# A Fourier layer with two feed-forward layers: the set-up ahead of the main loop written in another order, with four of its parts done in another way

## The chip, the cores and the metric

One NeuronCore of a Trainium2 chip. The metric is the time of one execution on the device, in microseconds (us), as the median over runs. The engines are called PE (TensorE), DVE (VectorE), ACT (ScalarE), POOL (GpSimd) and SP (SyncE, which only issues transfers here).

## The reference

```python
X = np.fft.fft(x, axis=1)          # x: (2, 3008, 256)
X = np.fft.fft(X, axis=2)
x = X.real.astype(np.float32).reshape(6016, 256)
h = x @ w_in                       # (256, 2048)
g = np.where(h >= 1, h, np.where(h <= -1, 0.0, (h + 1) ** 2 / 4))
x = (g @ w_out).astype(np.float32)
h = x @ w2_in
g = np.maximum(0.01 * h, h)
return (g @ w2_out).astype(np.float32)
```

The four weights arrive as float64 and are brought to float32 on the device, from their two 32-bit words. Every product with a main weight is made from a high and a low part of both factors (three products in place of one).

## The kernel before

**The set-up** (up to the first `step`) makes three things. (1) The first layer's weights w1 in 8 blocks: a load (`load_w1`, 512 KB), the conversion to float32 (`ToF32`: `begin` is two ACT passes, `exponent` one DVE pass L216, `join` two, `sign` L220 and `rest` L225), a product with the Fourier matrix of the 256 columns (`g_product`, PE), and the split of the result into high (`g_high`, ACT) and low (`g_low`, DVE) parts, `wa0` to `wa7`. (2) x, as 2 batches of 3 blocks: `load_x` brings one half of 512 KB by SP's queue, `add_x` adds the other half onto it by an accumulating transfer that POOL issues, `fold_x` (ten DVE passes and two or three on one column, L411 to L436) forms sums and differences. (3) The Fourier products over the 3008 positions: `even_product` (matrices `me0` to `me3`) and `odd_product` (matrices `mo0`, `mo1`), each in fp32 over the three blocks of a batch, into PSUM tiles `dc`/`ds` and `do`; then `odd_copy` and `odd_sum` join the odd halves, and `even_high`/`even_low`, `odd_high`/`odd_low` split all results into `bt0` to `bt7` (batch 0 has 0 to 3). The 129th frequency column goes other ways: `col_copy`, `col_even`, `col_even_out` (`ct` tiles by ACT), `col_row` (two row transfers out to DRAM and back spread over 128 partitions, issued by POOL), and for the weights `g_col` (many 2-column products) with `g_col_copy` into `g128`. `col_sign` flips signs in four `ct` tiles during later steps. `fill` and, in steps 1 to 3, the products into `full` serve no result.

**The main loop** has 128 steps of layer 1 and 128 of layer 2. Step n of layer 1 computes `p` (6 products), on DVE `aa`, two halves of `h` and a maximum `r`, on ACT three passes, then a high part `gh` (ACT) and a low part `gl` (POOL, L609); `second` of step n-4 (12 products into `acc`) follows `p` of step n on PE. The second weights w2 are converted too: blocks 0 to 3 in the set-up, 4 to 7 by a table of due steps (`plan_at`), with the low parts of 4 to 7 on POOL.

**The order** of the set-up is the list `ORDER`, written by hand: each item issues its instructions on its engines in turn, and every engine runs its own in that order. The tile pools add waits: a load into a reused buffer waits for the buffer's last reader. SP's loads are also numbered over eight completion counters, so that the ninth waits for the first to land, and so on; one waiting load holds back all behind it in SP's queue.

```python
def add_x(b, c):
    G.dma_start(out=xr[b, c], in_=xpq[b, c, 1], accum_op=ALU.add)
...
def sign(self):
    V.scalar_tensor_tensor(out=self.tmp, in0=self.high, scalar=-0x80000000, in1=self.tmp,
                           op0=ALU.bitwise_and, op1=ALU.bitwise_or)
```

Of the kernel before, what the change touches and what calls it, by code (L numbers as in the profile page):

```python
# [117 lines left out]
def _token_rows():  # L118

    i = np.arange(H4)  # L120
    rows = []
    for b in range(B):
        for k, neg in ((4 * i, 4 * (i + 1)), (4 * i + 2, 4 * i + 2),
                       (2 * i + 1, 2 * i + 1), (1503 - 2 * i, 1503 - 2 * i)):
            rows += [b * S + k, b * S + (S - neg) % S]
    return np.concatenate(rows)
# [4 lines left out]
load_w1 1, load_w1 4, load_x 0 0, load_cd, load_x 0 1, load_w1 2, load_x 0 2, w1_begin 1, load_w1 3,  # L131
w1_exponent 1, w1_begin 4, w1_join 1, w1_exponent 4, add_x 0 0, load_w1 0, g_product 1, fill 3, load_me 2,
w1_join 4, add_x 0 1, load_w1 6, g_product 4, fill 3, g_high 1, last_copy, load_me 3, load_mo 0, w1_begin 2,
g_low 1, load_mo 1, w1_exponent 2, g_high 4, add_x 0 2, w1_join 2, w1_begin 3, g_low 4, load_w1 7, g_product
2, fill 3, w1_exponent 3, w1_begin 0, w1_join 3, g_high 2, w1_exponent 0, load_w1 5, g_product 3, load_me 1,
g_low 2, w1_join 0, g_high 3, fold_x 0 0, g_product 0, w1_begin 6, g_high 0, g_low 0, load_x 1 0, col_copy 0
0, load_me 0, fold_x 0 1, even_product 0 1 0, g_col 1, load_w2 0, odd_product 0 0 0, g_col 4, w1_exponent 6,
even_product 0 1 1, g_col 2, col_copy 0 1, g_low 3, odd_product 0 0 1, w1_join 6, odd_product 0 1 0, g_col 0,
load_w2 1, fold_x 0 2, g_product 6, w1_begin 7, odd_product 0 1 1, g_high 6, w1_begin 5, w1_exponent 7,
odd_product 0 0 2, g_col 3, col_copy 0 2, g_low 6, w1_exponent 5, w1_join 7, add_x 1 0, odd_product 0 1 2,  # L140
g_col 6, odd_copy 0 0, w1_join 5, load_w2 2, load_x 1 1, odd_sum 0 0, load_w2 3, even_product 0 1 2, load_x 1
2, odd_high 0 0, odd_copy 0 1, g_product 5, odd_low 0 0, even_high 0 1, even_low 0 1, odd_sum 0 1,
even_product 0 0 0, g_high 5, fold_x 1 0, odd_high 0 1, even_product 0 0 1, add_x 1 1, even_product 0 0 2,
even_high 0 0, odd_low 0 1, odd_product 1 1 0, col_copy 1 0, even_low 0 0, add_x 1 2, col_row 0, odd_product 1 0 0, g_low
5, fold_x 1 1, even_product 1 0 0, g_col 5, g_product 7, fold_x 1 2, g_high 7, even_product 1 0 1, col_copy 1
1, odd_product 1 1 1, odd_product 1 0 1, g_low 7, w2_begin 0, even_product 1 0 2, g_col 7, w2_begin 1,
w2_exponent 0, col_copy 1 2, w2_exponent 1, col_even 0, even_high 1 0, w2_join 0, odd_product 1 0 2, even_low
1 0, col_even_out 0, w2_join 1, w2_begin 3, w2_exponent 3, w2_begin 2, even_product 1 1 0, odd_copy 1 0,
w2_exponent 2, odd_product 1 1 2, odd_sum 1 0, odd_high 1 0, odd_low 1 0, even_product 1 1 1, g_col_copy,
odd_copy 1 1, odd_sum 1 1, col_even 1, odd_high 1 1, odd_low 1 1, col_row 1, even_product 1 1 2, even_high 1 1, even_low  # L150
1 1, col_even_out 1, w2_high 0, step 0, w2_low 0, w2_high 1, w2_join 3, w2_low 1, w2_high 3, step 1,
w2_join 2, w2_low 3, w2_high 2, w2_low 2
# [5 lines left out]
def fnet_moe_kernel(ctx: ExitStack, tc: tile.TileContext, xpq, dft_e, dft_o, dft_d, pick,  # L158
# [39 lines left out]
    class ToF32:  # L198
# [4 lines left out]

        def load(self, w, j):
            self.raw = load_w(w, j)

        def begin(self):
# [15 lines left out]
        def rest(self):  # L223
            c = cv.tile([P, 512], I32, tag="cw", name="cw")
# [11 lines left out]
    def first_weights(j):  # L236
# [8 lines left out]
        def spill():  # L245
            c.rest()
# [45 lines left out]
        return ([("S", lambda: c.load(w3, j)), ("A", c.begin), ("V", c.exponent), ("V", c.sign), ("V", spill)],  # L292
# [3 lines left out]
    def second_weights(w, j, nm, engine, c):  # L296
# [6 lines left out]
        def low():  # L303
# [6 lines left out]

    with tc.manual_schedule():
# [5 lines left out]
        ev = pool("ev", 2, late, "right")  # L317
# [85 lines left out]
        def fold_x(b, c):  # L403
# [26 lines left out]
            x0, x1 = tc_[:, 2, P:P + 1], tc_[:, 3, P:P + 1]  # L430
            V.tensor_copy(tw_[:, 2, P - 1:P], x1)
            if c < 2:
                V.tensor_copy(tw_[:, 3, P - 1:P], x0)
            else:
                tt(tw_[:, 3, P - 1:P], x1, x0, ALU.subtract)
                V.scalar_tensor_tensor(out=tw_[:, 3, P - 1:P], in0=tw_[:, 3, P - 1:P], scalar=pk[:CH, 2:3],  # L436
                                       in1=x0, op0=ALU.mult, op1=ALU.add)
# [503 lines left out]
```

## Time and profile before

| | |
|---|---|
| median of 3 runs | 997.51 us (997.32 to 997.54) |
| the profiled execution: its time / its span | 996.57 us / 994.6 us |
| PE busy | 970.8 us (98%) |
| DVE / ACT / POOL busy | 63% / 71% / 50% |
| chain that ended last | PE 88%, DVE 6%, ACT 3%, DMA 2% |
| granted PE clock over the span | 0.995 |

The shares are means over a set-up of some 75 us and two long loops. The page's 40 slices show PE at 9 tenths in nearly all slices after the fifth; the first four hold the set-up, with DMA at 9, 9, 4, 2 tenths and DVE at 5 to 9. Times in the rows below are from the start of the span; a row of a timeline gives start, length, engine, line, operation, tiles and count, and in brackets the idle time before it and what ended it. A matmul of fp32 counts as two instructions in the trace.

### The profile page before, as it was taken

Reading aid. Unit: us, or ns where it says so; the run is one execution under the profiler, and the core shown is the slowest. Engines: PE = TensorE matmul, PEld = TensorE weight load, DVE = VectorE, ACT = ScalarE, POOL = GpSimd, SP = SyncE. Lnnn points to the kernel's source line nnn. Section 1 sums busy time; section 2 is a strip of 40 time slices with the busy share of each in tenths; the row PEclk is TensorE's granted clock in tenths of the full one; section 3 lists DMA queues with packets and bytes.
Section 4 is the critical chain, followed back from the end, with each engine's and each line's share of the span. In section 5 each row is a group of like instructions: output and inputs, shape, how many; then the busy total and the mean of one; then the engine's idle time right before and its main releaser. Section 6 shows DMA issues by size and latency. Waiting matters only on the chain.

```text
span 994.6 us, 14696 instructions
## 1 busy us (share of the span) xinstructions
PE 970.8 (98%) x5476; PEld 942.5 (95%) x5476; DVE 626.7 (63%) x1050; ACT 708.5 (71%) x1229; POOL 497.4 (50%) x291
## 2 busy tenths in 40 slices
PE   7997999999999999999999999999999999999998
PEld 5657899999999999999999999999999999999998
DVE  5989998888888988888877564252433423335211
ACT  4358888888888888878777676676666656666654
POOL 1013775555555656555520264554645546555444
PEclk9998999999999999999999999999999999999999
DMA  9942000110102010102364210101001010000000
GB/s 294 366 104 59 1 33 21 40 55 27 37 13 73 22 53 12 53 12 74 127 206 143 84 54 1 63 1 63 1 1 63 1 63 1 1 32 1 32 1 32
DMA packets 19464, 57.61 MB, mean 58 GB/s; under 512 B 2432, under 2 KB 2432, under 8 KB 19136
## 3 DMA queue, kind: packets, MB, share of 16 engines
q1 hardware_dynamic: 18000, 52.36, 14.9%
q0 software_dynamic: 1248, 3.92, 2.1%
q8 instruction: 43, 0.70, 0.3%
q10 hardware_dynamic: 144, 0.39, 0.1%
q14 instruction: 29, 0.24, 0.1%
HBM read 39.09 MB, written 14.42 MB: 54 GB/s over the span
## 4 chain that ended last, share of the span: by engine, by line
PE 88%; DVE 6%; ACT 3%; DMA 2%; issue 1%; POOL 0%; ACTq 0%; DVEq 0%; SPq 0%; POOLq 0%
PE acc L600 51%; PE x L589 12%; PE p L583 11%; PE v L589 6%; PE q L774 3%; PE y L589 3%; DMA rw<-in_w_dram 2%; DVE r L745 1%; DVE tw L220 1%; PE do L499 1%; DVE aa L732 1%; DVE h L735 1%; DVE h L736 0%; ACT gh L605 0%; DVE cw L225 0%
## 5 line engine op out<-in xcount | busy, mean ns | idle before, releaser
L609 POOL TENSOR_TENSOR gl<-s,gh 128x752 fp32r<-128x752 f32 x113 | 205.7, 1820 | 240.6 <-ACT gh L605 239.8
L609 POOL TENSOR_TENSOR gl<-r,gh 128x752 fp32r<-128x752 f32 x128 | 243.7, 1905 | 164.1 <-ACT gh L605 130.3
L600 PE MATMUL acc<-gh,wd 128*128 128x376 f32 x1024 | 287.7, 333 | 0.4 <-DVE o L630 0.4
L600 PE MATMUL acc<-gh,wb 128*128 128x376 f32 x1024 | 282.5, 337 | 0.2
L600 PEld LDWEIGHTS acc<-gh,wb 128*128 128x128 f32 x1024 | 187.8, 189 | 3.4 <-ACT r L742 2.2
L600 PEld LDWEIGHTS acc<-gh,wd 128*128 128x128 f32 x1024 | 187.0, 188 | 0.7 <-DVE o L630 0.7
L600 PE MATMUL acc<-gl,wb 128*128 128x376 f32 x512 | 172.7, 337 | 4.5 <-POOL gl L609 4.5
L600 PE MATMUL acc<-gl,wd 128*128 128x376 f32 x512 | 170.5, 333 | 0.0
L583 PE MATMUL p<-bt,wa 127*128 127x376 f32 (+3 forms) x768 | 154.9, 337 | 5.2 <-DVE h L736 5.2
L761 ACT ACTIVATE s<-s 128x752 f32<-128x752 f32 x112 | 75.8, 676 | 94.6 <-DVE s L838 94.6
L583 PEld LDWEIGHTS p<-bt,wa 128*128 128x128 f32 (+1 forms) x768 | 135.4, 189 | 6.1 <-issue 5.8
L745 DVE TENSOR_TENSOR r<-h,r 128x752 f32<-128x752 f32 x128 | 126.7, 990 | 0.1
L828 DVE TENSOR_TENSOR s<-v,bb 128x376 f32<-128x376 f32 x56 | 30.8, 550 | 152.2 <-PE v L589 152.1
L605 ACT CAST gh<-s 128x752 fp32r<-128x752 f32 x128 | 105.2, 822 | 15.0 <-PE acc L600 10.7
L738 ACT ACTIVATE r<-h 128x376 f32<-128x376 f32 x128 | 66.2, 517 | 64.0 <-DVE h L735 58.4
L749 ACT ACTIVATE r<-r 128x752 f32<-128x752 f32 x128 | 106.8, 834 | 4.1
L732 DVE SCALAR_TENSOR_TENSOR aa<-ct,g,p 128x376 f32<-128x376 f32 (+1 forms) x128 | 77.3, 604 | 44.4 <-PE p L583 44.1
L600 PEld LDWEIGHTS acc<-gl,wb 128*128 128x128 f32 x512 | 96.9, 189 | 7.3 <-POOL gl L609 7.3
L605 ACT CAST gh<-r 128x752 fp32r<-128x752 f32 x128 | 103.3, 807 | 0.2 <-PE q L774 0.2
L600 PEld LDWEIGHTS acc<-gl,wd 128*128 128x128 f32 x512 | 96.1, 188 | 0.0
L589 PE MATMUL x<-op,ws 128*128 128x376 f32 x336 | 75.8, 334 | 0.0
L589 PE MATMUL v<-op,ws 128*128 128x376 f32 x336 | 75.7, 333 | 0.0
(106 smaller groups left out, 1302.0 us busy)
## 6 DMA issues: line engine op xcount, KB each, us to landing
rw<-in_w_dram SPq DMA_DIRECT2D x32, 512.0 KB, 4.4
y<-o SPq DMA_DIRECT2D x16, 376.0 KB, 2.6
ry<-y SPq DMA_DIRECT2D x16, 376.0 KB, 3.9
out_dram<-o SPq DMA_DIRECT2D x15, 376.0 KB, 2.6
rf<-w3f SPq DMA_DIRECT2D x16, 256.0 KB, 2.8
x<-in_xpq_dram SPq DMA_DIRECT2D x6, 512.0 KB, 6.7
x<-in_xpq_dram POOLq DMA_DIRECT2D x6, 512.0 KB, 7.5
wt<-wc SPq DMA_DIRECT2D x8, 384.0 KB, 3.5
```

The lines of the kernel that those rows point to most:

```text
L583: T.matmul(p[:, j, :n], lhsT=w[:m, 2 * j + x, :], rhs=b[:m, 2 * j + y, :n], start=(a == 0), stop=(a == 2))
L589: T.matmul(bank[:, :H4], lhsT=w[:, x, :], rhs=y[:, z, :], start=start and a == 0, stop=a == 2, skip_group_check=not start)
L600: T.matmul(acc[k][:, :H4], lhsT=w[:, x, m * P:(m + 1) * P], rhs=y[:, t, :], start=(f == 0 and i == 0), stop=(f == NF - 1 and i == 2))
L605: A.copy(gh[n], gp[n])
L609: engine.tensor_tensor(out=gl[n], in0=gp.pop(n), in1=gh[n].bitcast(F32), op=ALU.subtract)
L732: V.scalar_tensor_tensor(out=aa[:, :w], in0=ct[u][:, :w], scalar=g128[:, f:f + 1], in1=p[:, 0, :w], op0=ALU.mult, op1=ALU.add)
L738: A.activation(r[:, 0], h[:, 0], HOLD, scale=240.0)
L745: V.tensor_tensor(out=g, in0=hp.pop(n - 1), in1=g, op=ALU.max)
L749: A.activation(r, r, AF.Square, scale=0.5 / 240.0, bias=0.5)
L761: A.activation(out, h, AF.Prelu, alpha=0.01)
L774: T.matmul(p[:, t, :H4], lhsT=block[:, x, :], rhs=ops[0][d][:, t, z, :], start=(a == 0), stop=(a == 5))
L828: V.tensor_tensor(out=h1[:, 1], in0=v[:, :H4], in1=bb, op=ALU.add)
```

## The change

- `ORDER` is another list (one line of it is shown).
- The first batch's second half of x is loaded by SP into a buffer `q` of its own (`load_q`), and DVE adds it (`sum_x`, one pass over 128x1024). The second batch still uses the accumulating transfer.
- Odd products use one matrix `mo0` for both kinds, with the blocks of the weights exchanged; the signs that this leaves go into the order of the output rows (`_token_rows`), and `col_sign` is gone.
- `even_product` takes a pair of banks from the pool of the odd products (`psum_pair`), all but the first.
- `sign` is gone: ACT's second pass of `begin` keeps the sign. The one-column passes of `fold_x` go to ACT (`col_copy`).
- `g_col` is replaced by transfers of one row of each `wa` to DRAM and back (`g_row`, `g_rows`, issued by POOL) and two products (`g_last`) that each fill half of `g128`.
- `col_row`'s transfers are issued by SP. Of batch 1, the odd product of the second kind (`do110`, `do111`) stands behind step 0.
- Low parts move: `odd_low` of (0, 0) and (1, 1) and the lows of w2's blocks 1 to 3 to POOL, those of blocks 4 to 7 to DVE. `full` is gone.

```diff
 ORDER = [s.strip() for s in """
-load_w1 1, load_w1 4, load_x 0 0, load_cd, load_x 0 1, load_w1 2, load_x 0 2, w1_begin 1, load_w1 3,
+load_x 0 0, load_q 0 0, load_w1 1, load_cd, load_q 0 1, load_w1 2, load_mo 0, w1_begin 1, load_x 0 1, sum_x
...
-            A.activation(t, t, AF.Copy, scale=2.0 ** -103)
+            A.activation(t, t, AF.Prelu, scale=2.0 ** -103, alpha=2.0 ** 32)
...
-        def sign(self):
-            V.scalar_tensor_tensor(out=self.tmp, in0=self.high, scalar=-0x80000000, in1=self.tmp,
-                                   op0=ALU.bitwise_and, op1=ALU.bitwise_or)
...
+        def load_q(b, c):
+            xq[b, c] = rq.tile([P, 1024], F32, tag="q", name=f"q{b}{c}")
+            nc.sync.dma_start(out=xq[b, c], in_=xpq[b, c, 1])
+
+        def sum_x(b, c):
+            V.tensor_tensor(out=xr[b, c], in0=xr[b, c], in1=xq.pop((b, c)), op=ALU.add)
...
+        def g_row(j):
+            G.dma_start(out=rows[j // 4][j % 4:j % 4 + 1], in_=wa[j][P - 1:P, :, 2:4, :].bitcast(F32))
+
+        def g_rows(i):
+            t = gr[i] = mo_p.tile([NF, P], F32, name=f"gr{i}")
+            G.dma_start(out=t, in_=rows[i].rearrange("j q e f -> (j q e) f"))
+
+        def g_last(i):
+            T.matmul(pgs["g128"][:, :NF // 2], lhsT=gr[i], rhs=pk[:NF, :], start=True, stop=True)
+            V.tensor_copy(g128[:, i * NF // 2:(i + 1) * NF // 2], pgs["g128"][:, :NF // 2])
...
-                pde[b, j] = (psum_one(f"dc{b}{j}"), psum_one(f"ds{b}{j}"))
+                if (b, j) == (0, 1):
+                    pde[b, j] = (psum_one(f"dc{b}{j}"), psum_one(f"ds{b}{j}"))
+                else:
+                    p = psum_pair(f"de{b}{j}")
+                    pde[b, j] = (p[:, 0], p[:, 1])
...
-            odd_matmuls(pdo[b, tr], P, lambda blk, lo, hi: w[lo:hi, 2 + blk], mo[tr], c)
+            odd_matmuls(pdo[b, tr], P, lambda blk, lo, hi: w[lo:hi, 2 + (1 - blk if tr else blk)], mo[0], c)
...
-                G.dma_start(out=row, in_=pdo[b, 1][h][P - 1:P, :])
+                nc.sync.dma_start(out=row, in_=pdo[b, 1][h][P - 1:P, :])
...
-            plan_at(3 * (j - 4), (0, "S", load), (1, "A", begin), (2, "V", exponent), (3, "V", w2c[j].sign),
-                    (4, "V", w2c[j].rest), (5, "A", to_high), (5, "V", to_low))
...
+            plan_at(3 * (j - 4), (1, "A", begin), (2, "V", exponent), (3, "V", join), (5, "A", to_high),
+                    (7, "V", to_low))
...
-                if n in (1, 2, 3):
-                    full = psum_one(f"full{n}")
-                    for _ in range(6):
-                        T.matmul(full[:, :H4], lhsT=wa[0][:, 0, 0, :], rhs=bt[0][:, 0, :H4], start=True, stop=True)
```

**The order on DVE, at the start of the program.** `tw` and `cw` are the two stages of a weight's conversion, `x`, `w`, `pc` and `xt` the stages of a fold, `q` the separate second half. Before:

```order
L216 TENSOR_SCALAR tw<-tw 128x512
L220 SCALAR_TENSOR_TENSOR tw<-rw,tw 128x512
L225 SCALAR_TENSOR_TENSOR cw<-rw,tw 128x512
L216 TENSOR_SCALAR tw<-tw 128x512
L220 SCALAR_TENSOR_TENSOR tw<-rw,tw 128x512
L225 SCALAR_TENSOR_TENSOR cw<-rw,tw 128x512
L388 TENSOR_TENSOR wa_170<-g_146,wa_170 128x2x128 x2
```

Now:

```order
L341 TENSOR_TENSOR x_120<-x_120,q_122 128x1024
L216 TENSOR_SCALAR tw<-tw 128x512
L221 SCALAR_TENSOR_TENSOR cw<-rw,tw 128x512
L412 TENSOR_TENSOR w_163<-x_120 126x508
L412 TENSOR_TENSOR x_120<-x_120 126x4x127
```

The first fold, which stood behind five weight conversions, now stands behind one.

**The order on POOL, from its last transfers of x to the first `gl`.** Before, only transfers stand ahead of the first `gl`:

```order
L548 DMA row_623<-bs_608 8x1x47
L550 DMA ct_625<-row_623 128x376
L609 ISA
L609 TENSOR_TENSOR gl<-r,gh 128x752 x4
```

Now (`rows`, `gr`: the row of the weights on its way out and back; `bt<-bs`: `odd_low`; `wb<-cw`: a low part of w2):

```order
L344 DMA x_348<-in_xpq_dram 128x1024
L376 DMA rows_109<-wa_284 2x1x256
L376 DMA rows_108<-wa_467 2x1x256
L543 ISA
L543 TENSOR_TENSOR bt_236<-bs_366,bt_236 128x376
L543 TENSOR_TENSOR bt_237<-bs_367,bt_237 128x376
L380 DMA gr_530<-rows_108 16x128
...
L297 TENSOR_TENSOR wb_640<-cw,wb_640 128x2x256
L297 TENSOR_TENSOR wb_642<-cw,wb_642 128x2x256
L297 TENSOR_TENSOR wb_646<-cw,wb_646 128x2x256
```

The `ISA` instruction and POOL's first arithmetic, which stood with the first `gl` in the main loop, now stand inside the set-up.

**The order on PE, up to the second `p`.** Before:

```order
L464 MATMUL dc11_583<-me2_154,xt12_512 128x376
L465 MATMUL ds11_584<-me3_174,xt12_512 127x376
L583 MATMUL p0_0_657<-bt0_423,wa0_259 128x378 x6
L583 MATMUL p0_1_682<-bt0_423,wa0_259 128x378 x6
L730 MATMUL full1_689<-bt0_423,wa0_259 128x376 x6
```

Now:

```order
L464 MATMUL de11_526<-me2_259,xt12_446 128x376
L465 MATMUL de11_526<-me3_241,xt12_446 127x376
L383 MATMUL g128_113<-pk_106,gr0_530 128x8
L479 MATMUL cc0_567<-me0_318,col_107 128x378 x3
L589 MATMUL p0_0_604<-bt0_355,wa0_467 128x378 x6
L499 MATMUL do110_622<-mo0_132,xt10_339 128x376 x2
L499 MATMUL do111_623<-mo0_132,xt11_401 128x376 x2
```

The odd product of the second kind of batch 1 (8 products) has moved from ahead of the first `p` to behind it, and the first product with `g128`'s transferred rows stands ahead of it.

## Rows read from the trace of the kernel before

**Rows 1.** Busy time by stretch (stretch, length; PE, PEld, DVE, ACT, POOL; clock, DMA share, GB/s)
```profile
5.90:75.20 69.30, 62.17 (x251) 41.94 (x250) 57.48 (x147) 31.43 (x72) 8.32 (x12) 0.98 0.81 254
12.00:24.00 12.00, 8.38 (x37) 6.76 (x36) 7.60 (x15) 4.68 (x11) 0.86 (x1) 0.95 1.04 278
28.00:40.00 12.00, 11.32 (x48) 7.86 (x50) 11.22 (x34) 3.10 (x7) 0.86 (x1) 1.00 1.01 414
93.10:131.60 38.50, 35.93 (x199) 34.44 (x199) 36.71 (x54) 30.93 (x53) 27.50 (x14) 0.98 0.00 1
300.00:400.00 100.00, 99.94 (x578) 99.07 (x577) 85.57 (x141) 84.18 (x139) 60.27 (x33) 1.00 0.12 40
```

**Rows 2.** Timeline of PE: `p` of steps 0, 5 and 16
```profile
73.63 2.52 PE L583 MATMUL p<-bt,wa 128*128 128x378 f32 x12
...
93.14 1.84 PE L583 MATMUL p<-bt,wa 128*128 128x378 f32 x6
...
131.66 1.20 PE L583 MATMUL p<-bt,wa 128*128 128x376 f32 x6
```

**Rows 3.** Timeline of DVE: a conversion, a fold's first and eleventh pass, the first `aa`
```profile
21.71 0.68 DVE L220 SCALAR_TENSOR_TENSOR tw<-rw,tw 128x512 int32<-128x512 int32 x1
...
23.04 0.68 DVE L411 TENSOR_TENSOR w<-x 126x508 f32<-126x508 f32 x1
...
26.64 0.15 DVE L431 COPY xt<-xt 126x1 f32<-126x1 f32 x1
...
75.21 0.60 DVE L732 SCALAR_TENSOR_TENSOR aa<-ct,g,p 128x378 f32<-128x378 f32 x1
```

**Rows 4.** Groups by shape, 0 to 125 us, DVE: a split's half; ACT: the two passes of `begin`
```profile
L543 DVE TENSOR_TENSOR bt<-bs,bt 128x376 fp32r<-128x376 f32 x4 | 2.0, 548 | 0.2
...
L212 ACT ACTIVATE tw<-rw 128x512 f32<-128x512 f32 x16 | 10.7, 672 | 12.4 <-DMA rw<-in_w_dram 8.2 <-DVE xt L411 4.1
L213 ACT ACTIVATE tw<-tw 128x512 f32<-128x512 f32 x16 | 10.1, 630 | 0.5
```

**Rows 5.** Timeline of POOL: accumulating transfers issued, and transfers of x awaited
```profile
7.90 1.04 POOL L340 DMA_DIRECT2D x<-in_xpq_dram  x1 [7.45 <-DMA x<-in_xpq_dram]
...
12.57 0.86 POOL L340 DMA_DIRECT2D x<-in_xpq_dram  x1 [1.79 <-DMA x<-in_xpq_dram]
```

**Rows 6.** Timeline of SP's queue: the issue of `mo0` and `mo1`
```profile
10.60 1.07 SPq L348 DMA_DIRECT2D mo<-in_dft_o_dram  x2
```

**Rows 7.** Transfers issued from 10 to 11 us: size, us to landing
```profile
mo<-in_dft_o_dram SPq DMA_DIRECT2D x1, 1128.0 KB, 19.1
```

**Rows 8.** Timeline of PE: a weight's product, four odd products, what follows
```profile
14.51 1.89 PE L368 MATMUL g<-cw,cd 128*128 128x256 f32 x8
...
58.74 2.69 PE L499 MATMUL do<-mo,xt 126*128 126x376 f32 x8
61.27 0.80 PE L464 MATMUL dc<-me,xt 126*128 126x378 f32 x2
```

**Rows 9.** POOL's queue, line 609: its configuration (count, least/mean/most ns, from and to)
```profile
L609 POOLq MODIFY_POOL_CONFIG  x2: 37/37/37, 79.1 to 79.2; - x2
```

**Rows 10.** Timeline of POOL: its first arithmetic, and line 609 behind line 305
```profile
87.50 1.97 POOL L609 TENSOR_TENSOR gl<-r,gh 128x752 fp32r<-128x752 f32 x1 [8.37 <-DVE r L745]
...
99.48 1.29 POOL L305 TENSOR_TENSOR wb<-cw,wb 128x512 fp32r<-128x512 f32 x1
100.76 2.48 POOL L609 TENSOR_TENSOR gl<-r,gh 128x752 fp32r<-128x752 f32 x1
```

**Rows 11.** Timeline of DVE: steps 6 to 10 of layer 1
```profile
99.68 1.90 DVE L745 TENSOR_TENSOR r<-h,r 128x752 f32<-128x752 f32 x1
101.50 2.29 DVE L220 SCALAR_TENSOR_TENSOR tw<-rw,tw 128x512 int32<-128x512 int32 x1
103.72 0.60 DVE L732 SCALAR_TENSOR_TENSOR aa<-ct,g,p 128x378 f32<-128x378 f32 x1
...
114.23 0.60 DVE L732 SCALAR_TENSOR_TENSOR aa<-ct,g,p 128x378 f32<-128x378 f32 x1
```

More of the change, by code (lines that the diff above doesn't have):

```diff
@@ L120, in _token_rows @@
     i = np.arange(H4)
+    odd = i % 2 == 1
     rows = []
     for b in range(B):
-        for k, neg in ((4 * i, 4 * (i + 1)), (4 * i + 2, 4 * i + 2),
-                       (2 * i + 1, 2 * i + 1), (1503 - 2 * i, 1503 - 2 * i)):
-            rows += [b * S + k, b * S + (S - neg) % S]
+        for k, neg, other in ((4 * i, 4 * (i + 1), False), (4 * i + 2, 4 * i + 2, False),
+                              (2 * i + 1, 2 * i + 1, odd), (1503 - 2 * i, 1503 - 2 * i, ~odd)):
+            k, neg = b * S + k, b * S + (S - neg) % S
+            rows += [np.where(other, neg, k), np.where(other, k, neg)]
@@ L136 @@
[L136 to L150, printed above, removed]
@@ new lines @@
+0 0, w2_begin 0, even_product 1 0 1, w1_exponent 7, col_copy 1 1, g_row 4, w1_join 7, w2_exponent 1,
+odd_product 1 0 2, g_product 7, load_w2 4, g_row 0, even_product 1 0 2, w2_join 1, odd_copy 1 0, odd_sum 1
+0, w2_begin 2, g_high 5, odd_low_g 0 0, even_high 1 0, even_product 1 1 0, w2_exponent 0, g_rows 0, w2_join
+0, g_high 7, even_product 1 1 1, odd_high 0 1, w2_begin 3, g_low 5, odd_low 0 1, g_low 6, g_low 7,
+w2_exponent 2, w2_join 2, col_even 1, w2_exponent 3, even_low 1 0, g_row 7, even_product 1 1 2, g_last 0,
@@ L153 @@
+col_even 0, odd_high 1 0, g_row 5, col_even_out 1, even_high 1 1, g_row 6, col_even_out 0, open_steps,
+odd_low 1 0, step 0, g_rows 1, odd_product 1 1 0, w2_join 3, even_low 1 1, odd_product 1 1 1, odd_product 1
+1 2, w2_high 3, w2_high 1, odd_copy 1 1, w2_high 2, w2_low_g 3, w2_low_g 1, odd_sum 1 1, w2_low_g 2, g_last
+1, w2_high 0, odd_high 1 1, odd_low_g 1 1, step 1, col_row 1, w2_low 0
 """.replace("\n", " ").split(",")]
@@ L245, in spill @@
         def spill():
-            c.rest()
+            c.join()
             t["dram"] = sp.tile([P, 512], F32, name=f"w3f{j}")
@@ L324, in fnet_moe_kernel @@
         rx = pool("rx", 3, early, "right")
+        rq = pool("rq", 2, early, "right")
         cd = me_p.tile([P, 2, 2, P], F32, name="cd")
-        pk = me_p.tile([P, 4], F32, name="pk")
-        last = me_p.tile([P, 2], FR, name="last")
+        pk = mo_p.tile([P, NF // 2], F32, name="pk")
         col = mo_p.tile([CH, 3, 2, B, P // B], F32, name="col")
-        xr, xt, w1c, me, mo, pgs, pde, pdo = {}, {}, {}, {}, {}, {}, {}, {}
+        xq, xr, xt, w1c, me, mo, pgs, pde, pdo = {}, {}, {}, {}, {}, {}, {}, {}, {}
+        rows = [sp.tile([4, 2, 2, P], F32, name=f"rows{i}") for i in range(2)]
+        gr = {}
         w2c = [ToF32() for _ in range(8)]
-        w2s = [second_weights(w2, j, "wb", V if j < 4 else G, w2c[j]) for j in range(8)]
+        w2c[2].home = w2c[3].home = ev
+        w2s = [second_weights(w2, j, "wb", w2c[j]) for j in range(8)]
         def load_x(b, c):
@@ L429, in fold_x @@
             tt(ts_[:, 1], pn[:, 0], pn[:, 1], ALU.add)
[L430 to L437, printed above, removed]
             xt[b, c] = (tc_, tw_)
         def col_copy(b, c):
-            A.copy(col[:, c, :, b, :], xt[b, c][0][:, 0:2, P:P + 1].to_broadcast([CH, 2, P // B]))
+            tc_, tw_ = xt[b, c]
+            for i in range(2):
+                A.copy(tw_[:, 2 + i, P - 1:P], tc_[:, 3 - i, P:P + 1])
+            A.copy(col[:, c, :, b, :], tc_[:, 0:2, P:P + 1].to_broadcast([CH, 2, P // B]))
         def both(c, j, lo=0, hi=CH):
```

119 lines of the change are left out of this document (54 added, 65 removed).

## The prediction, made before the changed kernel ran

> **What bounds the kernel now.** I read the busy times by stretch first. In the loop, between 300 and 400 us, PE works 99.94 of 100 us at a granted clock of 1.00 [rows 1]; nothing that the change touches lies there, and PE's work in it stays as it is. What can move is what stands ahead: the set-up, up to the first `aa` at 75.21 [rows 3], and the steps behind it. `p` of step 5 starts at 93.14 and that of step 16 at 131.66 [rows 2]: 38.5 us for eleven steps. Three steps on DVE, from `aa` at 103.72 to `aa` at 114.23, took 10.51, so 3.50 each [rows 11]. The loop's own pace I take as 3.1, six products of `p` and twelve into `acc` at some 0.17 each; eleven steps at it are 34.1, so 4.4 us of the stretch are lost. DVE is busy there for 36.71 of 38.5 us, PE for 35.93 [rows 1]: DVE holds PE up a little.
>
> In the set-up, between 5.9 and 75.2, DVE works 57.48 of 69.3 us and PE 62.17, but PE's time holds `fill`, `full` and stretched products; the DMA engines work at a share of 0.81 [rows 1]. So DVE's list is the first bound, and the loads that its parts wait for the second. The first fold starts at 23.04, behind the weight conversions [rows 3], though its x was awaited by 12.57 at the latest for its third part [rows 5]: the order, more than the data, makes it late.
>
> **DVE's list up to the first `aa`.** Removed: ten passes of `sign`. One and the L225 pass behind it took 1.33 from start to start (21.71 to 23.04, [rows 3]), so 0.67 each: 6.7. The fourteen one-column passes of the folds: 0.15 long [rows 3]; a pass's length reaches some 0.07 into the next one's start (99.68 + 1.90 is 101.58, the next starts at 101.50 [rows 11]), so 0.08 each: 1.1. One `odd_sum`, two `odd_low` and one `even_low`, eight halves that stand behind step 0 now or on POOL: 0.548 long [rows 4], 0.47 net: 3.8. Together 11.6. Added: three `sum_x` over 1024 elements, about twice the 508 that took 0.68 [rows 3]; 1.2 each (bounds 1.0 and 1.4): 3.6. One more join ahead of the first `aa`: 0.7. Net -7.3, which leaves 57.5 - 7.3 = 50.2 us of work.
>
> Idle time in the new order, item by item: DVE starts at about 6.0, as before; 2.2 until w1 block 1, third in SP's queue (the third thing awaited before came at about 7.9 [rows 5]), with two ACT passes of 0.672 and 0.630 [rows 4] behind it; 0.8 for the first `x01`, ninth load, put at 15.3; 0.5 for `x02`; 0.5 for an `es` copy behind a `begin` on ACT; 1.3 for the first accumulate of batch 1; 1.2 for `es10` behind a `begin` of w2; 1.2 for the high parts behind another; 0.9 for `ct0`. These are estimates of mine from the order and ACT's two passes: 8.6 in all. First `aa`: 6.0 + 50.2 + 8.6 = 64.8, against 75.2: **-10.4**.
>
> **The same from PE's side.** The even products of batch 0 wait for `me1`, now the last of the matrices. Up to it SP issues fifteen blocks of 512 KB, one of 256, `mo0` of 1128 KB [rows 7] and four of 567: 11.6 MB, with one accumulate 12.1. Before, eight loads or 3.4 MB were there by 12.57 [rows 5], and `mo0`, issued at 10.60 [rows 6] with 19.1 us to landing [rows 7], closed some 8.9 MB at 29.7: 0.32 MB/us between. By that the rest lands at 39.8; at 414 GB/s, reached between 28 and 40 [rows 1], at 33.6. I take 35.5, since batch 0 has no accumulates now. Behind it stand 26 fp32 products at 0.63 (four took 58.74 to 61.27), four weight products at 1.89 [rows 8], two column products of three each (3.8) and the first `p`, 1.20 [rows 2]: 16.4 + 7.6 + 3.8 + 1.2 = 29.0, so 64.5. The two sides agree; the late landing would cost 3.8.
>
> **POOL's start.** Before, POOL's configuration ran at 79.1, 37 ns twice [rows 9], and its first arithmetic at 87.50 after 8.37 of idle time, with 1.97 for a `gl` [rows 10]. Whether something unseen took place between cannot be read, since `r` came only then: up to 8.3 us would have been covered. Now both stand ahead of `odd_low` (0, 0), ready at about 51; behind it waits `odd_sum` (1, 0) on DVE (its tile for the sums is the one that POOL reads), and behind that PE's last even product pair, whose banks it frees. Bounds 0 and 8.3; no row is near either, so the middle, 4.1: `odd_low` ends at 57.4 and not 53.3, and as the wait takes the place of part of the 1.2 for `es10`, **+2.9** at the first `aa`. The Trainium skill (GPSIMD Engine Reference, 2.1 Instruction dispatch) says that the first call after a configuration also pays a load of about 6 us that no instruction of the profile shows; no row here shows or excludes it, and by it the term would be some +4.8 and the sum 1.9 higher.
>
> **DVE beside POOL.** A DVE pass with two operands that meets arithmetic on POOL stretched: L745 took 1.90 at 99.68 while `wb` ran on POOL from 99.48 to 100.77, and an L220 took 2.29 (0.68 alone [rows 3]) while `gl` ran to 103.24 [rows 10, 11]. Seven such POOL instructions are added in the set-up and the first step. Bounds: 0, since only the half ahead of step 0 meets a full DVE, and 6, a POOL instruction's length of about 1 us for six; **+1.5**, near the lower, since DVE idles in part beside them.
>
> **Steps 5 to 16.** Of every three steps, `sign` goes (0.7), the 1.29 of `wb` on POOL becomes one DVE pass of about 0.7, and the collision that cost 1.6 (2.29 for 0.68) and one of about 0.8 go with it in part. Three steps lose 10.51 - 9.3 = 1.2. Bounds 0 and -4.4 for the eleven; **-2.5**, rather over the half, since the collisions with `gl` stay.
>
> **What I cost at nothing.** `full` and the two-column products: PE waits for DVE or `me1` there anyway, so without that cover they would give a further gain of some 3 us, not a loss. `do110` and `do111` behind step 0: eight fp32 products, 5 us of PE, while PE waits for the first `gh` and `gl` (`gl` came 14 us after the first `p` [rows 2, 10]); without that cover +5. The sign's multiplier inside `begin`, and copies on ACT in place of DVE: ACT is busy for 31.43 of 69.3 us [rows 1]. The row transfers on SP hold back w2's blocks 5 to 7 until the sums are there; those are wanted from step 4 on, about 83; the time of one such transfer is that of any, up to 19.1 [rows 7]. `col_sign` stood in ACT's idle time. The even products in the other banks remove one wait and add the one named under POOL.
>
> **Sum.** -10.4 + 2.9 + 1.5 - 2.5 = -8.5. The profiled execution took 996.6, so 988.1; the median of the runs shown is 997.5, 0.94 more, so **989.0**. Best ends (POOL at once, no collisions, 4.4 from the steps): -14.8, or 982.7.
>
> **Rivals.**
> (A) POOL starts at once and the steps run at 3.1: -2.9 and -1.9, so 984.2, down to 982.7 without collisions. For it: two configurations of 37 ns, a first `gl` of ordinary length. Against: DVE is nearly full in the steps.
> (B) POOL's start takes longer than the middle, 6 us or more, hidden before: `odd_low` (0, 0) ends at 59.3 or later, 1.9 later than summed, all of it on the path: 990.9, and at 8.3 us 993.2. For it: the idle 8.37 would have covered that [rows 10]. It is what the skill's page on GPSIMD, 2.1, would give.
> (C) The order gains less: ACT's list is late at the four places where I gave it 0.5 to 1.2, or `me1` lands at 39.8 (+3.8): 992.5 to 996.
> (D) Nothing to measure, within 2.0 us, the 0.2% that a measurement here can tell from no change: the gain ahead of step 0 is given back because w2 or `gl` is late behind it. Between `p` of step 0 at 73.63 and that of step 5 at 93.14 [rows 2] the five steps took 19.5 where 15.5 would do, so something there waits already.
> (E) Slower: the loads. With x, its second half and the weights in flight, the transfers may keep the 254 GB/s of the whole set-up, as in 12 to 24, where the engines were full (share 1.04) at 278 [rows 1]. Then `me1` lands at 48.5 (12.1 MB at 0.254, and 1 for the start), and 29.0 behind it the first `aa` comes at 77.5, +2.3; with +1.5 and -2.5 that is 998.8. It decides from a landing at 46 to 47 on; above 49 it costs over 0.2%. Against: 414 GB/s from 28 to 40, and the accumulates that stood in 12 to 24 are gone.
>
> **Chances.** Forecast (987 to 990) 0.34, A 0.22, B 0.20, C 0.12, D 0.06, E 0.06. Below 982 and above 995 I leave out some 0.15: range 982 to 995. Faster by over 0.2%: forecast, A, B and most of C, 0.87; the same: D with a little of C, 0.07; slower 0.06.
>
> **What would show it.** Right: the first fold's passes from about 10.6; the second `sum_x` from about 15.3; the first even product near 35.5 behind `me1`; the first `aa` near 67 on DVE; `p` of step 16 some 8.5 earlier than 131.66. POOL's start: the gap between its configuration and its first arithmetic, and what ended the wait of `odd_sum` (1, 0). Collisions: lengths of L221 and L745 beside POOL. Wrong: a first `aa` at 70 or later (C or E; the landing of `me1` tells which), or a first `aa` at 67 with step 16 at 128 or later (D).

## The result, and the profile after

The changed kernel takes 981.92 us (median of 4 runs, 981.42 to 983.23), the kernel before 997.52 beside it: a ratio of 0.9834, 95% interval 0.9803 to 0.9865. That is 15.6 us faster, 7.1 more than the forecast of 989.0 and just below the stated range (982 to 995). The spans of the profiled executions are 994.6 and 978.4. Executions of the kernel before spread from 993.68 to 1002.56 over the whole study, so the single times of the experiments say little; they are read by stretches of their traces. One later execution of the changed kernel took 5421.77 us; its cause is open, and it is left out everywhere.

The first `aa` scatters too, and differences of less than 1 us there say nothing by themselves: five profiled runs with the changed kernel's set-up have it at 64.02, 64.14, 64.48, 64.79 and 65.03, and the latest of them was already 0.5 late in its first fold. The stretch from `p` of step 5 to `p` of step 16 repeats far better: 34.15 to 34.33 in both profiles of the changed kernel and in the six runs whose edit lies in the set-up alone.

Busy times by stretch, after (columns as in [rows 1]); the first ends at the first `aa`, the third runs from `p` of step 5 to `p` of step 16:

```profile
5.79:64.10 58.31, 55.79 (x216) 37.64 (x215) 51.06 (x119) 32.18 (x82) 9.90 (x15) 1.00 0.77 273
12.00:24.00 12.00, 11.72 (x48) 8.56 (x47) 11.06 (x27) 4.29 (x14) 1.61 (x2) 1.00 1.03 376
82.09:116.25 34.16, 34.16 (x199) 34.16 (x199) 33.16 (x55) 32.15 (x55) 21.78 (x12) 1.00 0.01 1
300.00:400.00 100.00, 99.93 (x577) 99.06 (x576) 84.04 (x138) 84.01 (x139) 59.28 (x33) 1.00 0.11 40
```

The main loop is as it was [rows 1]. In the third line PE is busy for all of 34.16 us, where it had 35.93 of 38.5. Timeline of PE, after: `p` of steps 0, 5 and 16, against [rows 2]:

```profile
62.53 1.51 PE L589 MATMUL p<-bt,wa 128*128 128x378 f32 x6
...
82.09 1.20 PE L589 MATMUL p<-bt,wa 128*128 128x378 f32 x6
...
116.25 1.20 PE L589 MATMUL p<-bt,wa 128*128 128x376 f32 x6
```

| stretch | before | after | difference | forecast |
|---|---|---|---|---|
| to the first `aa` | 75.21 | 64.14 | -11.07 | -10.4 + 2.9 + 1.5 = -6.0 |
| `p` of step 0 to `p` of step 5 | 19.51 | 19.56 | +0.05 | 0 |
| `p` of step 5 to `p` of step 16 | 38.52 | 34.16 | -4.36 | -2.5 |
| `p` of step 16 to the end of the span | 862.9 | 862.2 | -0.8 | 0 |

Timeline of DVE, after: the first fold (against 23.04 in [rows 3]), the second `sum_x`, the second half of `odd_sum` (0, 0), the three passes that stretched beside POOL ahead of the first `gl` (2.33, 1.54 and 1.46), an `aa` beside POOL that did not, the first `aa`, and a join in step 6:

```profile
9.47 0.68 DVE L412 TENSOR_TENSOR w<-x 126x508 f32<-126x508 f32 x1
...
14.29 1.23 DVE L341 TENSOR_TENSOR x<-x,q 128x1024 f32<-128x1024 f32 x1 [0.81 <-DMA x<-in_xpq_dram]
...
34.46 0.53 DVE L522 TENSOR_TENSOR bs<-es,do 128x376 f32<-128x376 f32 x1
...
50.48 2.33 DVE L216 TENSOR_SCALAR tw<-tw 128x512 int32<-128x512 int32 x1
...
64.14 0.61 DVE L734 SCALAR_TENSOR_TENSOR aa<-ct,g,p 128x378 f32<-128x378 f32 x1 [1.28 <-ACT ct L486]
...
70.24 0.60 DVE L734 SCALAR_TENSOR_TENSOR aa<-ct,g,p 128x378 f32<-128x378 f32 x1
...
71.79 1.54 DVE L747 TENSOR_TENSOR r<-h,r 128x752 f32<-128x752 f32 x1
73.26 1.46 DVE L297 TENSOR_TENSOR wb<-cw,wb 128x512 fp32r<-128x512 f32 x1
...
89.27 0.68 DVE L221 SCALAR_TENSOR_TENSOR cw<-rw,tw 128x512 int32<-128x512 int32 x1
```

POOL, after: the configuration at line 543 (columns as in [rows 9]), then the timeline of POOL:

```profile
L543 POOLq MODIFY_POOL_CONFIG  x2: 42/42/42, 50.5 to 50.5; - x2
```
```profile
49.97 0.51 POOL L376 DMA_DIRECT2D rows<-wa  x1 [11.86 <-DVE tw L216]
50.57 1.94 POOL L543 TENSOR_TENSOR bt<-bs,bt 128x376 fp32r<-128x376 f32 x2
...
67.79 3.80 POOL L297 TENSOR_TENSOR wb<-cw,wb 128x512 fp32r<-128x512 f32 x3 [3.70 <-ACT wb L293]
71.55 2.63 POOL L543 TENSOR_TENSOR bt<-bs,bt 127x376 fp32r<-127x376 f32 x2
77.15 1.99 POOL L615 TENSOR_TENSOR gl<-r,gh 128x752 fp32r<-128x752 f32 x1 [2.98 <-DVE r L747]
...
89.67 1.96 POOL L615 TENSOR_TENSOR gl<-r,gh 128x752 fp32r<-128x752 f32 x1 [1.12 <-ACT gh L611]
```

The configuration ran at 50.5 and the first arithmetic at 50.57, two halves of 376 columns in 1.94; a `gl` of 752 columns took 1.99 later. Nothing stands between configuration and arithmetic.

Timeline of PE, after: the places where it waits between 27.7 and 60:

```profile
28.80 0.87 PE L464 MATMUL dc<-me,xt 126*128 126x376 f32 x2 [1.04 <-DMA me<-in_dft_e_dram]
...
35.09 0.87 PE L464 MATMUL de<-me,xt 126*128 126x378 f32 x2 [0.59 <-ACT tw L212]
...
54.65 0.87 PE L464 MATMUL de<-me,xt 126*128 126x376 f32 x2 [0.58 <-DVE bs L522]
```

The first even products of all, with the matrices `me2` and `me3`, start at 28.80, those of unit 0 at 35.09 (forecast 35.5). The wait ahead of 35.09 is put down to an ACT pass, but its banks are those that `odd_sum` (0, 0) on DVE leaves at 34.99 (34.46 and 0.53); in the run of the attempt at a faster kernel below, the same wait is put down to `odd_sum` itself. From 27.7 to `p` of step 0 PE waits for 2.2 us in all.

### The profile page after: what moved, and what is told of

Read it like the earlier page. It is cut to its first block, busy times and chain, and to the rows that moved or that the text cites. A ratio compares the mean times of both kernels' runs of the same rounds, so it can differ in the third digit from the quotient of the medians.

```text
span 978.4 us, 14606 instructions
## 1 busy us (share of the span) xinstructions
PE 963.2 (98%) x5442; PEld 937.0 (96%) x5442; DVE 603.9 (62%) x1005; ACT 707.9 (72%) x1236; POOL 492.1 (50%) x293
## 4 chain that ended last, share of the span: by engine, by line
PE 91%; DVE 2%; ACT 2%; POOL 0%; issue 0%; ACTq 0%; DVEq 0%
PE acc L606 53%; PE p L589 13%; PE x L595 12%; PE v L595 6%; PE q L776 3%; PE y L595 3%; ACT gh L611 0%; PE do L499 0%; PE cc L479 0%; DVE aa L734 0%; ACT r L740 0%; ACT r L751 0%; DVE h L737 0%; DVE r L747 0%; PE de L464 0%; POOL gl L615 0%
## 5 line engine op out<-in xcount | busy, mean ns | idle before, releaser
L615 POOL TENSOR_TENSOR gl<-r,gh 128x752 fp32r<-128x752 f32 x128 | 239.2, 1869 | 164.7 <-ACT gh L611 136.8
L611 ACT CAST gh<-s 128x752 fp32r<-128x752 f32 x128 | 105.2, 822 | 15.6 <-PE acc L606 10.9
```

The lines of the kernel that those rows point to most:

```text
L611: A.copy(gh[n], gp[n])
L615: engine.tensor_tensor(out=gl[n], in0=gp.pop(n), in1=gh[n].bitcast(F32), op=ALU.subtract)
```

## The experiments

The theory after the result: the set-up follows DVE's list, with PE's list behind the even matrices close to it; POOL starts without delay; and steps 5 to 16 were held up by DVE passes that met POOL's work. Rivals: PE's list or the loads alone; `sign` alone, or the moved low part alone, in the steps.

**Steps 5 to 16: sign back in blocks 4 to 7.**

```diff
+        for c in w2c[4:]:
+            c.signed = True
 ...
         def join(self):
+            if self.signed:
+                self.sign()
```

> The changed kernel with the DVE sign pass back in the conversions of w2's blocks 4 to 7 alone (steps 3, 6, 9 and 12 of layer 1). Stretch looked at: p of step 5 to p of step 16, 38.5 us before, 34.2 after. Theory (DVE was overfull there, and sign, the low part moved from POOL to DVE, and their collisions each had a share): three passes of 0.67 fall in the stretch, 1.0 of them goes into DVE's idle time, so 35.2 to 36.2. Rival 1 (sign alone was the overload): 37.5 or more. Rival 2 (only POOL's low part and its collisions were): 34.2 to 34.5. Up to the first aa no change (64.1).

Measured: p of step 5 at 82.44, of step 16 at 124.99: 42.55, so 8.4 more, four times the theory's upper end and more than the kernel before took. By the number it is rival 1 that came in (37.5 or more); the next run tests what that rival says of the low part. First `aa` at 64.79, within the scatter. Timelines of DVE and of POOL in this run:

```profile
92.11 0.68 DVE L220 SCALAR_TENSOR_TENSOR tw<-rw,tw 128x512 int32<-128x512 int32 x1
92.83 2.19 DVE L227 SCALAR_TENSOR_TENSOR cw<-rw,tw 128x512 int32<-128x512 int32 x1
94.94 0.59 DVE L742 SCALAR_TENSOR_TENSOR aa<-ct,g,p 128x378 f32<-128x378 f32 x1
```
```profile
92.51 1.95 POOL L623 TENSOR_TENSOR gl<-r,gh 128x752 fp32r<-128x752 f32 x1 [1.12 <-ACT gh L619]
97.57 2.11 POOL L623 TENSOR_TENSOR gl<-r,gh 128x752 fp32r<-128x752 f32 x1 [3.10 <-ACT gh L619]
```

`sign` itself took 0.68, but it pushed the join behind it onto `gl`: the join began 0.32 after `gl` did and ended 0.56 after `gl` ended. That is 2.19 for a pass of 0.68. All three joins of the stretch went that way (2.19, 2.18, 2.21). In the changed kernel the join starts 0.40 ahead of `gl` and takes 0.68 (89.27 and 89.67 above). The next `gl` then came late too (3.10 of idle time on POOL). Three signs at 0.7 and three joins 1.5 longer are 6.6 of the 8.4 us; that the rest is what the late `gl` holds back is argued, not shown.

**Steps 5 to 16: low parts back on POOL.**

```diff
-                    (7, "V", to_low))
+                    (5, "V", lambda to_low=to_low: to_low(G)))
```

> The changed kernel with the low parts of w2's blocks 4 to 7 back on POOL, in the fifth step after their start as before the change. Stretch p of step 5 to p of step 16. Theory: DVE loses three passes of 0.68 but two passes in every three steps stretch beside POOL, as the 1.90 and 2.29 did before: 35.0 to 36.5. Rival 1 (sign alone was the overload): 34.2. Rival 2 (POOL's low part alone was): 38 or more.

Measured: 82.22 to 119.26, 37.04, or 2.9 more; a little over the theory's range, and both rivals fall: the move of the low part has a share of its own beside `sign`. POOL's `wb` stood from 99.37 to 101.36 and the join beside it, from 100.13, took 1.78: again it ended 0.55 after POOL did.

**Steps 5 to 16: the two parts alone, in the kernel before.**

```diff
-            plan_at(3 * (j - 4), (0, "S", load), (1, "A", begin), (2, "V", exponent), (3, "V", w2c[j].sign),
-                    (4, "V", w2c[j].rest), (5, "A", to_high), (5, "V", to_low))
+            plan_at(3 * (j - 4), (0, "S", load), (1, "A", begin), (2, "V", exponent), (3, "V", w2c[j].rest),
+                    (5, "A", to_high), (7, "V", to_low))
```

(with the sign kept by ACT's second pass and the low part on DVE for these four blocks)

> The kernel before with only the two parts for w2's blocks 4 to 7: no sign pass, low part on DVE two steps later. Theory: p of step 5 to p of step 16 takes 34.2 to 34.8 and not 38.5, the first aa stays at 75.2, the time falls by 3.7 to 4.4. Rival (the steps became short because the new set-up leaves other buffers and a different phase): 37 or more.

Measured: first `aa` at 75.08; p of step 5 at 93.01, of step 16 at 127.91: 34.90 (0.1 above the theory's range) where the kernel before took 38.52. The span is 990.6, 4.0 below 994.6. So 3.6 of the 4.4 us in the steps come from these two edits and not from the new set-up. Each of the two alone in the kernel before was not run.

**The low part on POOL at 50.57.**

(the items of `ORDER` that differ; in the new order `odd_low 0 0` stands between the other two)

```diff
-odd_low_g 0 0,
+w1_join 7, odd_low 0 0, w2_exponent 1,
```

> The changed kernel with odd_low (0, 0) on DVE, behind the join of w1's block 7, and not on POOL. Theory (POOL starts at once, and beside its 1.94 us a DVE pass of 0.42 took 2.33): DVE takes 0.95 for the two halves and gets the 1.9 back, odd_sum (1, 0) is 0.9 earlier, PE's wait of 0.58 for its bank goes, the first aa comes at 63.4 to 63.8 in place of 64.1. Rival (DVE's list is the bound and POOL's pass was free): 64.9 to 65.1.

Measured: first `aa` at 63.54, 0.6 earlier, as the theory has it; p of step 16 at 115.87. The 0.6 is less than the scatter of the first `aa`, but here it can be placed: PE's starts agree with those of the changed kernel to 0.01 from 35.1 to 53.3, and then its wait of 0.58 is gone (54.05 in place of 54.65). Timelines of DVE and of PE in this run:

```profile
50.67 1.00 DVE L544 TENSOR_TENSOR bt<-bs,bt 128x376 fp32r<-128x376 f32 x2
51.59 0.42 DVE L217 TENSOR_SCALAR tw<-tw 128x512 int32<-128x512 int32 x1
```
```profile
54.05 0.87 PE L465 MATMUL de<-me,xt 126*128 126x376 f32 x2
```

The L216 pass that took 2.33 beside POOL takes 0.42 again, which pays for the two halves. Moving 0.95 us of work to POOL had cost DVE 1.9. Its time, 979.74 in one execution, cannot be told from the changed kernel's.

**The set-up: sign back in its twelve conversions** (as in the first run, with `signed` set for w1's blocks and w2's first four).

> The changed kernel with the DVE sign pass back in the twelve conversions of the set-up, ten of them ahead of the sum that frees PE's last banks: 6.7 us more on DVE. Theory (PE's own list bounds the set-up from 29 us on, DVE follows closely with some 4 us of idle time ahead of that sum): first aa at 66.5 to 68.5 in place of 64.1. Rival 1 (DVE's list is the bound and has no slack that helps): 70.5 to 71. Rival 2 (the loads bound it): 64.1 to 64.8.

Measured: first `aa` at 71.14, 7.0 later, just above rival 1's range; the theory's range falls. But that the 7.0 is so near the ten passes' 6.7 is partly luck. Some idle time did take in 2.2 of them (the waits of 0.81 and 1.43 for x are gone); against that, the first conversion was ready 0.8 later, and PE idled for a join that met POOL's work in place of the L216 pass. Timeline of DVE, then of PE, in this run:

```profile
54.42 2.45 DVE L227 SCALAR_TENSOR_TENSOR cw<-rw,tw 128x512 int32<-128x512 int32 x1
```
```profile
56.92 3.33 PE L381 MATMUL g<-cw,cd 128*128 128x256 f32 x8 [2.26 <-DVE cw L227]
60.05 1.19 PE L473 MATMUL de<-me,xt 126*128 126x378 f32 x2
```

After those 2.26 us of idle time the weight product took 3.33 for its 1.99; the granted clock between 58 and 64 was 0.76, so part of that stretch ran at the lower of the two levels (1.2 and 2.4 GHz).

**The set-up: the first batch's x by accumulating transfers.**

(parts of `ORDER`)

```diff
-load_x 0 0, load_q 0 0, load_w1 1
+load_x 0 0, load_w1 1
...
-sum_x 0 1
+add_x 0 1, add_x 0 2
```

> The changed kernel with the first batch's second half of x added by accumulating transfers, as before the change, in the new order; no sum_x on DVE (3.7 us less). Theory (the early first fold is what the order is built on): the first fold starts at 15 to 19 in place of 9.5, and the first aa comes at 66 to 70. Rival 1 (from the landing of the even matrices on PE's list decides, what lies ahead has slack): 63.6 to 64.6. Rival 2 (DVE's list decides, 3.7 us are gained): 61 to 63.

Measured: first fold at 14.45 (the transfer was issued at 4.79 and POOL's next wait for it ended at 15.42), first `aa` at 70.43, 6.3 later although DVE had 3.7 us less to do. A little beyond the theory's range in both; the rivals fall. The added DVE passes are worth their time because the folds wait less: ahead of the first batch's three folds DVE waited 6.18, 2.25 and 2.86 for x, in the changed kernel 0.81 once its first block had come. Timeline of DVE in this run, the first fold:

```profile
14.45 0.69 DVE L413 TENSOR_TENSOR w<-x 126x508 f32<-126x508 f32 x1 [6.18 <-DMA x<-in_xpq_dram]
```

**The row transfers on POOL.**

```diff
-                nc.sync.dma_start(out=row, in_=pdo[b, 1][h][P - 1:P, :])
+                G.dma_start(out=row, in_=pdo[b, 1][h][P - 1:P, :])
```

(and the same for the way back)

> The changed kernel with the row transfers of the 129th column issued by POOL and not by SP. Theory (costed at nothing: no engine of the chain waits for either queue): first aa at 64.1 and p of step 5 at 82.1, both within 0.4. Rival (POOL's waits for the sums hold back the transfers of the weights' rows and the low parts behind them): later by 1 or more. Other rival (SP's held-back loads of w2 cost something in steps 3 to 8): p of step 16 earlier by 0.5 or more.

Measured: first `aa` at 65.30, p of step 5 at 86.72, of step 16 at 120.89: 1.2, 4.6 and 4.6 later. The theory of "nothing" falls by the steps; the 1.2 at the first `aa` is hardly more than its scatter. Timeline of POOL in this run:

```profile
75.29 0.53 POOL L556 DMA_DIRECT2D row<-bs  x1
77.17 0.58 POOL L558 DMA_DIRECT2D ct<-row  x1 [1.35 <-DMA row<-bs]
77.75 0.52 POOL L556 DMA_DIRECT2D row<-bs  x1
80.95 0.56 POOL L558 DMA_DIRECT2D ct<-row  x1 [2.69 <-DMA row<-bs]
81.53 6.02 POOL L615 TENSOR_TENSOR gl<-r,gh 128x752 fp32r<-128x752 f32 x3
```

Two round trips through DRAM, each with a wait on POOL, stand ahead of the first `gl`, which starts at 81.53 and not at 77.15. On SP only loads of w2 stand behind them. The other rival falls: nothing came earlier.

**Even products of unit 0 in banks of their own.**

```diff
-                if (b, j) == (0, 1):
+                if (b, j) in ((0, 1), (0, 0)):
```

> The changed kernel with the even products of unit 0 in single banks of their own and not in a pair of the odd ones' banks. Theory (the bank, not the data, is what then holds PE): the second of them waits until the low parts of unit 1 have left their banks at about 38.5 in place of 35.8, and the first aa is 1.5 to 3 later than 64.1. Rival (the banks never mattered in this order): 64.1 within 0.3.

Measured: the second product starts at 38.22 after 3.27 of idle time (for the low parts of unit 1), first `aa` at 68.30, 4.2 later: the place is the theory's, the price above its range. Other even products in banks of their own were not run. Timeline of PE in this run:

```profile
38.22 0.90 PE L465 MATMUL ds<-me,xt 126*127 126x378 f32 x2 [3.27 <-DVE bt L473]
```

**The last even matrix half a megabyte later.**

```diff
-load_me 1, fold_x 1 0, load_x 1 2,
+fold_x 1 0, load_x 1 2, load_me 1,
```

> The changed kernel with the load of the last even matrix behind the last block of x in SP's queue (0.5 MB later, some 1.3 us at 0.4 MB/us). Theory (DVE's list bounds the set-up, the matrix is there when its banks come free at 35.0, with little to spare): first even product of unit 0 at 35.6 to 36.4 in place of 35.1 and first aa later by 0.3 to 1.0, as PE's list behind it has only 0.6 us of idle time. Rival (the matrix came well ahead): 64.1 within 0.2. Rival (the loads are the bound alone): later by 1.3 or more.

Measured: first `aa` at 65.02, but all of this run is later by 0.4 from the first fold on (9.91). The first of the two products starts at 35.55, and the second waits for the matrix. Timeline of PE in this run:

```profile
37.19 0.90 PE L466 MATMUL de<-me,xt 126*127 126x378 f32 x2 [0.76 <-DMA me<-in_dft_e_dram]
```

The edit moved the load further than 1.3 us: the block of x ahead of it waits for its buffer, so SP issued the matrix at 28.1 and not at 23.2. In the changed kernel it had 12.0 us to landing, so it came at some 35.2 to 35.7, and its product started at 35.80: it is just in time there. But a price at the first `aa` is not shown. The attempt below leaves the set-up alone, ran on the same chip and was as late in its first fold (9.98): its second product started at 36.30, 0.9 ahead of this one's 37.19, and its first `aa` came at 65.03, the same. PE's wait for `odd_sum` (1, 0), 0.77 there, is gone here: that slack took the delay in. So the theory holds for the product and not for the first `aa`. Of the rivals, the first is right in the price and wrong in its reason, and the second falls.

**An attempt at a faster kernel.** The pass on w2's block 0 (1.46 at 73.26) stood between steps 1 and 2.

```diff
-step 1, col_row 1, w2_low 0
+step 1, col_row 1
...
+        plan_at(2, (0, "V", w2s[0][6]))
```

> The changed kernel with the low part of w2's block 0 on DVE in step 2, behind the maximum of step 1, where it stood ahead of step 2 and took 1.46 beside POOL. Theory (between the first aa and the first acc the steps wait for DVE alone): first gl at 75.7 to 76.2 in place of 77.15, p of step 16 at 114.8 to 115.5 in place of 116.25. Rival (ACT's high part or PE's odd products hold the steps): 116.0 to 116.4.

Measured: p of step 16 at 117.30; the theory falls, and the rival's number is missed too. But 0.9 of the delay lies ahead of the edit (first `aa` at 65.03, within the scatter). From the first `aa`, `p` of step 5 comes after 16.02 us (17.95 in the changed kernel) and `p` of step 16 after 52.27 (52.11, and 51.54 in its second profile): what is gained up to step 5 is lost behind it. Timelines of DVE, POOL and PE in this run:

```profile
76.87 2.29 DVE L298 TENSOR_TENSOR wb<-cw,wb 128x512 fp32r<-128x512 f32 x1
79.08 0.60 DVE L736 SCALAR_TENSOR_TENSOR aa<-ct,g,p 128x378 f32<-128x378 f32 x1
```
```profile
76.65 1.96 POOL L616 TENSOR_TENSOR gl<-r,gh 128x752 fp32r<-128x752 f32 x1 [1.60 <-DVE r L749]
```
```profile
75.92 1.28 PE L590 MATMUL p<-bt,wa 128*128 128x378 f32 x6 [1.72 <-DVE h L740]
```

The first `gl` came earlier, and the moved pass met it: 2.29 in place of 1.46.

> The changed kernel again, for its time on the chip that also runs the next one: 981.4 to 983.2, first aa at 64.1, p of step 16 at 116.2, as both theories say.

Measured: 980.45 us (median of three runs, 979.84 to 980.84), first `aa` at 64.02, p of step 16 at 115.56: the time is 0.95 below the range expected, and `p` of step 16 is 0.6 early, all of it between `p` of step 0 and `p` of step 5.

> The changed kernel with odd_low (0, 0) on DVE and the low part of w2's block 0 in step 2. Theory (the two gains add): first aa at 63.5, p of step 16 at 114.4 to 115.1, 1.1 to 1.9 less than the changed kernel. Rival (the second gain falls to another wait): 115.7 to 116, 0.3 to 0.6 less.

Measured, on the same chip: 981.23 us (980.08 to 981.52, four runs), first `aa` at 63.68, p of step 16 at 115.94. The earlier `aa` is kept, and p of step 16 lies where the rival had it. But from the first `aa` on it took 52.3, as in the attempt before, and it is later than in the changed kernel's profile on this chip (115.56): the second edit brings nothing. No version found here beats the changed kernel by what can be measured.

## Why the prediction was wrong

**What bounds the kernel: right.** The loop did not move, DVE's list was the first bound of the set-up, and the two sides did come out together: DVE was busy for 51.06 us up to the first `aa` (forecast 50.2) and idle for 7.3 (8.6); PE's first product of unit 0 came at 35.09 (35.5), and from there to the first `aa` it took 29.05 us (29.0). Two things in this agreement are luck. The 51.06 hold 1.9 of stretch beside POOL that the 50.2 do not, so the work itself was some 1 us less. And the last matrix did land near 35.5 (35.2 to 35.7), but it held up nothing: the first product of unit 0 doesn't need it and waited for banks that DVE leaves.

**The base term, -10.4: right, if some 1.3 short.** The first `aa` moved by -11.07, with one collision in it that cost 0.6, so -11.7 without; the scatter of the first `aa` is nearly as large as the difference. One reading behind it was loose: by 12.57 only the first halves of x were awaited. The second halves, by accumulating transfer, take longer: issued at 4.79, one let the fold start at 14.45 in the run above.

**POOL's start, +2.9: the first step that failed.** I took the middle of two bounds because no row of before could decide, and it was the lower bound: the arithmetic followed the configuration within 0.1 us, here and in eight other traces, and took no longer than a `gl` of the same size. The Trainium skill (GPSIMD Engine Reference, 2.1 Instruction dispatch) gives about 6 us for the first call to a freshly loaded kernel, which I took the work behind the configuration to be; the trace shows no such time between the two. Whether this configuration loaded anything, no run shows. With 0 the sum falls to -11.4. This is the first half of rival A.

**DVE beside POOL, +1.5: the mechanism right, the size too large ahead of the first `aa`.** One pass stretched there, by 1.9; with the low part back on DVE, which then works 0.95 more, the first `aa` came 0.6 earlier. The other two (0.6 and 0.8) lie in the steps up to 5, whose length is unchanged.

**Steps 5 to 16, -2.5: the second step that failed.** It came to -4.36, the whole loss, as in the second half of rival A. I counted `sign` as 0.7 per three steps and left the collisions with `gl` standing. They did not stay. The runs show that `sign` costs far more by what it pushes: one DVE pass that slips behind the start of `gl` waits for its end. Without it and without POOL's low part, the join starts ahead of `gl` and keeps its 0.68; only the maximum `r` still stretches (1.35 at 88.00). Put back alone into the changed kernel, `sign` costs 8.4 and the low part on POOL 2.9; both edits together, in the kernel before, gave 3.6 of the 4.4.

So both halves of rival A came true, which had a chance of 0.22 beside the forecast's 0.34; the time came in 0.8 below its lower end (982.7).

**Costed at nothing.** The row transfers on SP: right as a cost, but what the move spares was not seen; on POOL's queue in this order they would have been 4.6 us worse. The cover that I named for `do110` and `do111` held in sum: `p` of step 0 to `p` of step 5 took as long as before. `col_sign`, which I left out as idle time of ACT, may be the place of some 0.3 (steps 17 and 20 were 3.33 and 3.61 long before, 3.1 and 3.48 after); no run tests it. The rest of the last 0.8 is open; the conversions of the later weights lost their `sign` in that stretch too.

**The sum.** With the three terms behind the base at their measured size it would have been -10.4 + 0 + 0.6 - 4.4 = -14.2, or 983.3, within the range. By the profiles the rest is the base term's 1.3 and the 0.8 behind step 16; their spans differ by 16.2 where the medians differ by 15.6. Rivals B, C, D and E did not occur: E's transfers ran at 376 GB/s between 12 and 24, not 278. The range was too narrow at its low end, where both failed terms lie on the same side.

The gains of the parts don't add up: undoing `sum_x`, `sign` or the banks of unit 0 alone costs 6.3, 7.0 and 4.2 us at the first `aa`, 17.5 together, while the whole change gains 11.1. Each is the price of breaking an order that was written around all of them, not what the part brought.

## What to carry to other kernels

A DVE pass with two tiles in SBUF that begins while POOL is in its arithmetic may end only after POOL does, and one that begins ahead of it kept its length here; so look at the order in which the two start, not at their busy shares, before moving work to POOL or adding a short pass ahead of one that now just misses it. A transfer that waits for another transfer belongs on a queue behind which nothing on the path stands. Before a difference is put down to an edit, look how far the same stretch scatters in runs that leave it alone, and where in the trace the difference begins. Where two unknown terms of a sum can both be nothing, the range has to reach to the sum with both at nothing.

## What the runs showed of the hardware that was not expected

Beside POOL's arithmetic, DVE's passes over tiles in SBUF did not slow down in proportion but waited: 0.68 became 2.19, ending 0.56 after POOL (sign in the steps), 1.78, ending 0.55 after (low parts on POOL), 2.29, ending 0.55 after (block 0 in step 2); a pass with one operand of 0.42 became 2.33, ending 0.30 after (the changed kernel). `aa`, which reads PSUM for one of its operands, kept its 0.60 (70.24, beside POOL's work from 67.79). The Trainium skill (GPSIMD Engine Reference, 8 Key points) names contention of POOL with VectorE, on the SBUF interfaces that they share, for DVE instructions with two SBUF inputs or in a two-port mode. The traces agree for the passes with two tiles in SBUF, and add that here all but some 0.13 us of the pass's length is paid behind POOL's end; for the pass with one operand no row names a mode.

For that pass the order of the two starts is not the rule. In the changed kernel it began 0.09 ahead of POOL's arithmetic, and with the row transfers on POOL 0.51 ahead, while POOL still issued a transfer, and both times it ended 0.3 after POOL. In two other runs it began after POOL's first half had begun (by 0.15 with the accumulating transfers, by 0.30 with unit 0 in banks of its own); there it took 1.2 and ended before POOL's second half did. Beside transfers that POOL only issues it kept its 0.42 (at 60.53 in the changed kernel). What holds it stays open. Timelines of DVE and of POOL in the run with the row transfers on POOL:

```profile
51.23 2.74 DVE L216 TENSOR_SCALAR tw<-tw 128x512 int32<-128x512 int32 x1
```
```profile
51.74 1.94 POOL L543 TENSOR_TENSOR bt<-bs,bt 128x376 fp32r<-128x376 f32 x2
```

PE's clock: in the changed kernel PE was idle for 3.11 us ahead of `p` of step 4, and those six products took 2.23 us; the granted clock between 62 and 84 was 0.84, a mean of the two levels of 1.2 and 2.4 GHz. With block 0's pass moved, the idle time there was 1.72, the six took 1.28 (75.92 above) and the clock stayed at 1.00. What the lower clock cost in the end is not shown: that run gained 1.9 up to step 5 and lost it to another collision behind. Timeline of PE, after:

```profile
76.42 2.23 PE L589 MATMUL p<-bt,wa 128*128 128x378 f32 x6 [3.11 <-DVE h L738]
```
